# Four small statistic tiles of a two-layer attention and mixture kernel are given 128 bytes a partition each

## The chip, the cores and the metric

The kernel runs on one core of a Trainium2 chip. The metric is the time of one execution on the device in microseconds (us), and lower is better.

## The reference

Attention over 4 batches, 8 heads, 576 positions and 64 features; four heads see a local window of 32 positions, the other four every 32nd position. Its result, 2304 tokens by 512 features, goes through two gated layers of width 1536.

```python
scores = scale * np.matmul(q, k.transpose(0, 1, 3, 2))
scores = np.where(masks[None, :, :, :], scores, -1000000000.0)
attn = np.exp(scores - np.max(scores, axis=-1, keepdims=True))
attn = attn / (np.sum(attn, axis=-1, keepdims=True) + 1e-09)
x = np.matmul(attn, v)                  # then as 2304 tokens x 512
...
x = (x @ w_a) * (x @ w_b) @ w_out       # first layer, "moe"
gate = 1.0 / (1.0 + np.exp(-(x @ w_gate)))
out = gate * (x @ w_val) @ w_out        # second layer, "moe2"
```

## The kernel before, in words

**Precision.** Matmuls of the two layers run on fp32 words in one pass. Each operand is split into a high and a low part, and a product is three matmuls: high by high, low by high, high by low.

**Memory.** Almost all of the on-chip memory is cut into 17 zones (`REGIONS`, L68 to L73): `w0` to `w11` of 12,288 bytes a partition, `x12` to `x15` of 8,192, `h16` of 4,096. The function `at` (L364) gives each zone a tile of its own, and a zone is used anew in three phases; the names in the profile are `w4p` and so on, without the number of the phase. One large tile, `rest` (L361), holds everything else of size. The statistic tiles `nm0`, `nm1`, `nm2` (negated row maxima and sums of the local heads, L573) and `sm0` (the same of the strided heads, L799) are small tiles of their own, made by `buf` (L383). Tiles stand in a partition in the order in which the program first asks for them.

**First part, about 24 to 510 us.** Five tiles of tokens: four of 512 columns (4 batches by 128 positions) and a last one of 256. The tokens of a tile lie in `x12` to `x15` and are the moving operand; block k of the first layer's weights (k = 0 to 11, 128 hidden features each) lies in zone `wk` and is the stationary one. For each tile and each k the engine runs 24 matmuls at L923 (the products with `w_a` and `w_b`) and, one block later, 12 at L1013 (the output product, which moves the hidden values in `h16`). The same zone's weights are loaded for each matmul anew. Between them stand the small matmuls and transposes of the next tile's attention (L563, L604, L618, L877), whose operands lie in `rest`. The strided heads are computed by VectorE alone (L781, L787, L844, L851); the results are transposed at L877 and written to `x13` and `x15`.

**Second part, about 510 us to the end.** The second layer is done in products of 2 by 2 blocks with seven multiplications instead of eight (`seven`, L1276). All its matmuls are at L1292, with 384 columns. In its first stage tokens and their sums in `w0` to `w3`, `w6` to `w9`, `w11` to `w15` and others are moving, weights in `w4`, `w5`, `w10` and `w3` are stationary; in its last stage the zones change parts again, with weights in `w3`, `w4`, `w5`, `w7`, `w10` and `x12` to `x15`.

**Order.** A planner (`Plan`, with costs and due times) writes the instructions of each engine in a fixed order when the program is built. It knows zones and rings by number, and not the size of a small tile or an address.

```python
v = tiles[r][1][:, a - r[0]:a - r[0] + n]                            # L376, at(): a place in a zone
return sb.tile(shape, dtype, tag=f"{ring}{s}", name=f"{ring}{s}")    # L387, buf(): nm0 to nm2, sm0
```

Of the kernel before, what the change touches and what calls it, by code (L numbers as in the profile page):

```python
# [18 lines left out]
HL = H // 2  # L19
# [3 lines left out]
P = 128  # L23
# [322 lines left out]
def attention_moe_kernel(ctx, tc, qkv, sq, sk, sv, w1, w2, mask, ident, out):  # L346
# [17 lines left out]
    def at(a, n, phase=FIRST, dtype=F32):  # L364
        r = region_of(a)
        if r is None:
            v = rest[:, a - F0:a - F0 + n]
        else:
            if tiles.get(r, (None,))[0] != phase:
                name = f"{('w', 'x', 'h')[(r[0] >= X0) + (r[0] >= H0)]}{REGIONS.index(r)}"  # L370
                tiles[r] = phase, sb.tile([P, r[1]], F32, tag=name, name=f"{name}p{phase}")
            v = tiles[r][1][:, a - r[0]:a - r[0] + n]
        return v if dtype == F32 else v.bitcast(dtype)
# [9 lines left out]
    def buf(op, ring, shape, dtype=F32):  # L383
        s = op.slot[ring][0]
        if ring in PLACE:
            return at(PLACE[ring] + s * RINGS[ring][1], shape[1], FIRST, dtype)
        return sb.tile(shape, dtype, tag=f"{ring}{s}", name=f"{ring}{s}")  # L387
# [136 lines left out]
    def attention(g, key, banks, first, war, load=(), held=None, last=True):  # L524
# [44 lines left out]
        def blocks(a):  # L569
            return a.rearrange("p (b k) -> p b k", b=g.nb)  # L570

        def top(op):
            nm = buf(op, "nm", [P, 2 * HL])  # L573
            x["nm"], x["sm"] = nm[:, :g.nb], nm[:, HL:HL + g.nb]
            DVE.tensor_reduce(out=x["nm"], in_=blocks(x["s"]), op=ALU.max, axis=AX.X)  # L575
            DVE.tensor_scalar_mul(x["nm"], x["nm"], -SCALE)  # L576
# [81 lines left out]
        else:  # L658
            a = add("PE", nb * 162, qk, [lq, z] + war, key, take=ring(("c", es)), free=ring(("qk", lq)))
        used(a, [eq, ek])  # L660
        b = add("DVE", dve(w) + 200, top, [a], key + ST, take=[("nm", (0, 1, 2))])
        c = add("ACT", nb * (act(WB) + 186), exp, [b], key + 2 * ST,
                free=[("bank", z)])
# [29 lines left out]
    def strided(i, key, length, start, war):  # L693
        first = i == 0
        tq, t0 = TILES[i] // STRIDE, i * TB // STRIDE
# [100 lines left out]
                reds.append(reads(add("DVE", dve(nh * n * D), reduce, [m, fi], w, free=free), m))  # L796

        def stat(op):
            return buf(op, "sm", [P, HL * 4])[:, :HL * tq]  # L799

        def wide(a):
            return a.unsqueeze(2).to_broadcast([P, HL * tq, n1])
# [1 line left out]
        def top(op):  # L804
            x["m"] = stat(op)
            DVE.tensor_reduce(out=x["m"], in_=s3(), op=ALU.max, axis=AX.X)
# [787 lines left out]
```

## Time and profile before

| | |
|---|---|
| runs | 914.01 us (median of 3; 913.92 to 914.92) |
| span of the profiled execution | 912.5 us, first to last instruction |
| TensorE matmul busy | 903.8 us, 99% |
| TensorE weight load busy | 806.1 us, 88% |
| VectorE busy | 655.6 us, 72% |
| ScalarE busy | 404.7 us, 44% |
| granted TensorE clock | 1.000 of full speed over the whole run |

For the profiled execution the page gives its span alone, and no time of its own; 914.01 - 912.5 = 1.5 us of a run lie outside the span. Matmuls overlap one another, so the record of one is longer than the step from its start to the start of the next: that step is what a stream of matmuls costs, and it is read from rows that give a start, a length and a count.

### The profile page before, as it was taken

What the parts mean: (1) busy time and instruction counts of PE and PEld (TensorE: products, weight loads), DVE (VectorE), ACT (ScalarE), POOL (GpSimd) and SP (SyncE); (2) the same over time, 40 slices, a digit from 0 to 9 for tenths busy, and PEclk for the clock granted to TensorE, in tenths of its full rate; (3) what the DMA queues carried; (4) which work ended last, traced back from release to release, by engine and by line L of the source; (5) the groups of instructions that cost most, each with busy time, mean ns of one, the idle gap of its engine ahead of it and who ended that gap; (6) DMA issues with size and microseconds to landing.
All of it is one profiled execution on the core that took longest, in us unless ns stands there. A gap on an engine that the chain in (4) does not pass through costs nothing.

```text
span 912.5 us, 13664 instructions
## 1 busy us (share of the span) xinstructions
PE 903.8 (99%) x5170; PEld 806.1 (88%) x5170; DVE 655.6 (72%) x1078; ACT 404.7 (44%) x843; POOL 11.8 (1%) x23
## 2 busy tenths in 40 slices
PE   8999999999999999999999999999999999999998
PEld 4678887888888887888899999999999999999998
DVE  7999988998999879811328886675768458659481
ACT  5775644411242113311236655564656445435351
POOL 4000000000000000000000000000000000000000
PEclk9999999999999999999999999999999999999999
DMA  9666564311342123300034333645574588953401
GB/s 318 197 228 220 189 195 137 90 44 59 85 136 71 53 64 119 118 1 1 0 117 148 106 123 114 226 149 186 196 242 162 198 292 323 386 165 114 165 16 62
DMA packets 62513, 132.67 MB, mean 145 GB/s; under 512 B 5872, under 2 KB 37232, under 8 KB 61552
## 3 DMA queue, kind: packets, MB, share of 16 engines
q1 hardware_dynamic: 62160, 131.60, 42.9%
q8 instruction: 40, 0.66, 0.3%
q14 instruction: 25, 0.20, 0.1%
q10 hardware_dynamic: 288, 0.21, 0.1%
HBM read 97.19 MB, written 34.60 MB: 144 GB/s over the span
## 4 chain that ended last, share of the span: by engine, by line
PE 96%; DVE 3%; DMA 0%; issue 0%; ACT 0%; SPq 0%; DVEq 0%
PE bank L1292 43%; PE bank L923 33%; PE bank L1013 17%; PE bank L618 1%; PE bank L563 1%; PE bank L604 1%; DMA w11p<-sk 0%; PE bank L877 0%; DVE s L787 0%; DVE nm L575 0%; DVE rest L491 0%; DVE w11p L781 0%; DVE w8p L851 0%; DVE w9p L851 0%; DVE x14p L630 0%
## 5 line engine op out<-in xcount | busy, mean ns | idle before, releaser
L947 ACT CAST h16p<-rest 128x512 fp32r<-128x512 f32 (+1 forms) x60 | 34.7, 578 | 149.0 <-PE bank L1013 142.9
L1304 DVE TENSOR_TENSOR rest<-bank,rest 128x384 f32<-128x384 f32 x84 | 46.2, 555 | 58.4 <-PE bank L1292 33.5
L943 DVE TENSOR_TENSOR rest<-bank,rest 128x512 f32<-128x512 f32 (+1 forms) x60 | 38.1, 635 | 57.0 <-PE bank L923 56.3
L1065 ACT COPY rest<-bank 128x512 f32<-128x512 f32 (+1 forms) x60 | 32.6, 543 | 95.7 <-PE bank L923 95.5
L1310 ACT COPY rest<-bank 128x384 f32<-128x384 f32 x84 | 40.1, 479 | 69.3 <-PE bank L1292 69.2
L951 DVE TENSOR_TENSOR h16p<-rest,h16p 128x512 fp32r<-128x512 f32 (+1 forms) x60 | 38.2, 636 | 32.7 <-PE bank L1013 27.6
L844 DVE TENSOR_TENSOR rest<-rest,s 128x320 f32<-128x320 f32 (+13 forms) x56 | 51.5, 920 | 0.9
L781 DVE TENSOR_TENSOR rest<-rest 128x320 f32<-128x320 f32 (+13 forms) x56 | 51.5, 919 | 0.9
L787 DVE TENSOR_REDUCE s<-rest 128x5 f32<-128x320 f32 (+13 forms) x56 | 51.2, 914 | 1.2
L851 DVE TENSOR_REDUCE rest<-rest 128x64 f32<-128x320 f32 (+13 forms) x56 | 51.2, 914 | 1.0
L1202 DVE SCALAR_TENSOR_TENSOR rest<-rest 128x512 uint32<-128x512 uint32 x36 | 24.6, 687 | 9.5 <-ACT rest L1195 9.4
L482 ACT ACTIVATE rest<-rest 128x512 f16<-128x512 bf16 x36 | 28.4, 793 | 6.8 <-DMA rest<-w 6.4
L1195 ACT ACTIVATE rest<-rest 128x512 f16<-128x512 bf16 x36 | 28.0, 790 | 4.9 <-DMA rest<-w 4.8
L1375 DVE TENSOR_TENSOR rest<-bank,rest 128x384 f32<-128x384 f32 x36 | 20.0, 556 | 12.2 <-PE bank L1292 11.4
L1314 ACT COPY bank<-bank 128x384 f32<-128x384 f32 x42 | 19.5, 465 | 19.6 <-PE bank L1292 19.1
L1369 ACT ACTIVATE rest<-bank 128x384 f32<-128x384 f32 x36 | 17.7, 491 | 23.2 <-PE bank L1292 23.2
L491 DVE SCALAR_TENSOR_TENSOR rest<-rest 128x512 uint32<-128x512 uint32 x36 | 24.4, 684 | 0.9 <-ACT rest L482 0.9
L581 ACT ACTIVATE rest<-bank,nm 128x96 f32<-128x96 f32 x56 | 18.3, 339 | 12.0 <-DVE nm L576 10.4
L1369 ACT ACTIVATE rest<-rest 128x768 f32<-128x768 f32 x18 | 15.2, 845 | 14.0 <-DVE rest L1304 13.7
L1292 PE MATMUL bank<-w8p,w10p 128*128 128x384 f32 x100 | 20.8, 335 | 0.0
L1292 PEld LDWEIGHTS bank<-w8p,w10p 128*128 128x128 f32 x100 | 17.7, 188 | 0.0
L1292 PE MATMUL bank<-x15p,w3p 128*128 128x384 f32 x88 | 17.6, 335 | 0.0
(500 smaller groups left out, 2426.9 us busy)
## 6 DMA issues: line engine op xcount, KB each, us to landing
rest<-w SPq DMA_DIRECT2D x72, 511.8 KB, 4.0
h2d<-rest SPq DMA_DIRECT2D x18, 768.0 KB, 4.1
rest<-qkv SPq DMA_DIRECT2D x12, 416.0 KB, 4.0
w2p<-h2d SPq DMA_DIRECT2D x12, 384.0 KB, 4.3
w0p<-h2d SPq DMA_DIRECT2D x12, 384.0 KB, 5.4
w1p<-h2d SPq DMA_DIRECT2D x12, 384.0 KB, 4.9
out<-rest SPq DMA_DIRECT2D x24, 192.0 KB, 1.8
x2d<-rest SPq DMA_DIRECT2D x16, 256.0 KB, 2.0
```

The costliest lines, as they stand in the source:

```text
L781: engine[op.eng].tensor_tensor(out=product(op, n), in0=x["k", h][:, :, :n, :], in1=x["q"][h // 2][:, e:e + nh, j:j + 1, :].to_broadcast([P ...
L787: DVE.tensor_reduce(out=weights_of(h, j, n), in_=x["p", op.deps[0]], op=ALU.add, axis=AX.X)
L844: engine[op.eng].tensor_tensor(out=product(op, n, "p (h d t) -> p h d t"), in0=x["v", h][:, :, :, :n], in1=weights_of(h, j, n).unsqueeze(2 ...
L851: DVE.tensor_reduce(out=xs[:, j, e:e + nh, :], in_=x["p", op.deps[0]], op=ALU.add, axis=AX.X)
L923: PE.matmul(x[tag][:, :n], ww[:, c * P:(c + 1) * P], xx(c), start=(u == 0 and c == chunks[0]), stop=(u == last and c == chunks[-1]),)
L943: DVE.tensor_tensor(out=x["g"], in0=x["b"][:, :n], in1=x["g"], op=ALU.mult)
L947: ACT.copy(out=x["hh"], in_=x["g"])
L951: DVE.tensor_tensor(out=x["hl"], in0=x["g"], in1=r32(x["hh"]), op=ALU.subtract)
L1013: PE.matmul(ps[:, :n], ww[:, m * P:(m + 1) * P], x[xx], start=start, stop=stop)
L1292: PE.matmul(bank_of(where), at(*lhs(a, (0, 1, 0)[q], c), F32R), at(*rhs(b, (0, 0, 1)[q], c), F32R), start=p in OPENS and (q, c) == units[0 ...
L1304: DVE.tensor_tensor(out=at(*o), in0=bank_of("Z"), in1=at(*a), op=ALU.add)
L1310: "ACT", act2(NS), lambda op: ACT.copy(out=at(*o), in_=bank_of("Y")), [ops[after]], key - 20))
```

## The change

The four small tiles are asked for with 32 words (128 bytes) a partition: `nm0` to `nm2` had 8 words (32 bytes), `sm0` had 16 (64 bytes). The parts of them that are used stay the same.

```diff
         def top(op):
-            nm = buf(op, "nm", [P, 2 * HL])
+            nm = buf(op, "nm", [P, 32])
             x["nm"], x["sm"] = nm[:, :g.nb], nm[:, HL:HL + g.nb]
...
         def stat(op):
-            return buf(op, "sm", [P, HL * 4])[:, :HL * tq]
+            return buf(op, "sm", [P, 32])[:, :HL * tq]
```

The instructions of every engine are the same in both programs, in the same order (PE, DVE, ACT, POOL and SP alike). What differs is where tiles begin. Byte addresses within a partition, of the built programs:

| tile | before | after | before, modulo 128 | after, modulo 128 |
|---|---|---|---|---|
| rest | 3072 | 3072 | 0 | 0 |
| w11, w10, w9, w7, w6, w8, w5 | 43392 to 117120, in this order, in steps of 12288 | same | 0 | 0 |
| nm0 | 129408 | 129408 | 0 | 0 |
| nm1 | 129440 | 129536 | 32 | 0 |
| sm0 | 129472 | 129664 | 64 | 0 |
| nm2 | 129536 | 129792 | 0 | 0 |
| w4 | 129568 | 129920 | 32 | 0 |
| x12, x14, x13, x15 | 141856 to 166432, steps of 8192 | 352 bytes more | 32 | 0 |
| w0, w1 | 174624, 186912 | 352 bytes more | 32 | 0 |
| h16 | 199200 | 199552 | 32 | 0 |
| w2, w3 | 203296, 215584 | 352 bytes more | 32 | 0 |

Every operand of L923, L1013 and L1292 begins at its zone's start plus a multiple of 512 bytes, so it has its zone's remainder.

## Rows read from the trace of the kernel before

**Rows 1.** The page, part 1: busy time, share of the span, instructions.
```profile
PE 903.8 (99%) x5170; PEld 806.1 (88%) x5170; DVE 655.6 (72%) x1078; ACT 404.7 (44%) x843; POOL 11.8 (1%) x23
```

**Rows 2.** The page, part 4: the chain that ended last, by engine and line.
```profile
PE 96%; DVE 3%; DMA 0%; issue 0%; ACT 0%; SPq 0%; DVEq 0%
PE bank L1292 43%; PE bank L923 33%; PE bank L1013 17%; PE bank L618 1%; PE bank L563 1%; PE bank L604 1%; DMA w11p<-sk 0%; PE bank L877 0%; DVE s L787 0%; DVE nm L575 0%; DVE rest L491 0%; DVE w11p L781 0%; DVE w8p L851 0%; DVE w9p L851 0%; DVE x14p L630 0%
```

**Rows 3.** Line L1013, 195 to 455 us: min/median/max ns, first and last start.
```profile
L1013 PE MATMUL bank<-h16p,w8p x36: 392/397/400, 222.4 to 438.4; 128*128 128x512 f32 x36
...
L1013 PE MATMUL bank<-h16p,w0p x24: 389/389/499, 258.7 to 368.6; 128*128 128x512 f32 x24
...
L1013 PE MATMUL bank<-h16p,w3p x24: 389/389/392, 286.9 to 396.1; 128*128 128x512 f32 x24
```

**Rows 4.** The chain in order of time, third tile: start us, us, what.
```profile
222.56 2.81 PE bank L1013 x12
225.37 5.63 PE bank L923 x24
...
271.68 5.44 PE bank L923 x24
...
287.06 2.72 PE bank L1013 x12
```

**Rows 5.** Line L1013, 457 to 508 us, the tile of 256 columns.
```profile
L1013 PE MATMUL bank<-h16p,w3p x12: 283/283/283, 477.2 to 478.6; 128*128 128x256 f32 x12
...
L1013 PE MATMUL bank<-h16p,w8p x12: 277/280/282, 498.4 to 499.7; 128*128 128x256 f32 x12
```

**Rows 6.** The chain in order of time, the tile of 256 columns.
```profile
474.52 2.88 PE bank L923 x24
477.40 1.44 PE bank L1013 x12
...
498.58 1.41 PE bank L1013 x12
499.98 2.82 PE bank L923 x24
```

**Rows 7.** Groups by form, 565 to 910 us: out<-moving,stationary xcount | busy us, mean ns.
```profile
L1292 PE MATMUL bank<-w8p,w10p 128*128 128x384 f32 x100 | 20.8, 335 | 0.0
L1292 PE MATMUL bank<-w9p,w4p 128*128 128x384 f32 x82 | 16.3, 339 | 0.0
L1292 PE MATMUL bank<-x15p,w3p 128*128 128x384 f32 x76 | 15.3, 335 | 0.0
...
L1292 PE MATMUL bank<-w6p,w5p 128*128 128x384 f32 x72 | 14.5, 336 | 0.0
...
L1292 PE MATMUL bank<-w0p,w10p 128*128 128x384 f32 x36 | 7.2, 336 | 0.0
```

**Rows 8.** Timeline of PE, 705 to 708 us: start us, us, what.
```profile
705.10 1.20 PE L1292 MATMUL bank<-w8p,w10p 128*128 128x384 f32 x6
706.14 1.23 PE L1292 MATMUL bank<-w8p,w4p 128*128 128x384 f32 x6
707.20 1.20 PE L1292 MATMUL bank<-w8p,w10p 128*128 128x384 f32 x6
```

**Rows 9.** The chain in order of time, the second part.
```profile
510.58 44.14 PE bank L1292 x252
559.58 349.59 PE bank L1292 x1996
```

**Rows 10.** Timeline of DVE before the second tile's transposes: start, us, what, [idle].
```profile
125.45 0.69 DVE L951 TENSOR_TENSOR h16p<-rest,h16p 128x512 fp32r<-128x512 f32 x1 [0.79 <-PE bank L1013]
...
131.01 0.69 DVE L943 TENSOR_TENSOR rest<-bank,rest 128x512 f32<-128x512 f32 x1 [0.22 <-PE bank L923]
131.62 0.68 DVE L851 TENSOR_REDUCE rest<-rest 128x64 f32<-128x512 f32 x1
```

**Rows 11.** Timeline of PE at those transposes.
```profile
132.68 0.60 PE L877 MATMUL bank<-idt,rest 128*128 128x128 f32 x4
```

**Rows 12.** Timeline of PE, 558 to 560 us.
```profile
558.32 0.62 PE L1292 MATMUL bank<-w2p,w4p 128*128 128x384 f32 x2 [0.48 <-ACT w4p L1245]
559.58 0.97 PE L1292 MATMUL bank<-w2p,w4p 128*128 128x384 f32 x4 [0.64 <-DVE w4p L1248]
```

## The prediction

> **What bounds the kernel now.** I read the busy times first: the matmul engine is busy for 99% of the span and VectorE for 72% [rows 1]. The chain that ended last says the same with an order: 96% of it is PE, and three lines, L1292, L923 and L1013, make 93% [rows 2]. So the time is a number of matmuls times the step from one to the next, and an edit matters if it changes that step. This edit removes, adds and moves no instruction; it moves addresses. The question is thus whether the trace of before shows a step that depends on the address. It can, since before it holds both kinds of zone: `w5` to `w11` begin at a multiple of 128 bytes ("on 0"), all zones from `w4` on, by place, 32 bytes past one ("on 32").
>
> The first look is at one line with one moving operand. At L1013 `h16` (on 32) moves through weights of every zone, 512 columns each. With weights on 32 the record of a matmul lasts 389 ns at its median, which is also its minimum; with weights on 0 it lasts 397 [rows 3]. The records overlap, so I check the step itself in the chain: twelve matmuls with `w8` take 2.81 us, 234.2 ns each, and twelve with `w3` 2.72 us, 226.7 each; the blocks of 24 at L923 take 5.63 and 5.44 us, 234.6 and 226.7 [rows 4]. (Which block is which follows from the order: an output block at L1013 stands between the products of the next two blocks. The row at 222.56 is that of `w8`, by rows 3, so the 24 behind it belong to `w10`; the row at 287.06 is that of `w3`, and the 24 at 271.68 are its products.) **Pairs of unlike remainder cost 7.5 ns more here.**
>
> With 256 columns it is the other way, by less: `w3` 283 ns and `w8` 280 [rows 5], in the chain 1.44 and 1.41 us for twelve, 2.88 and 2.82 for 24: 120.0 against 117.5 each [rows 6].
>
> Line L1292, 384 columns, has all four combinations. Both on 0: 335 and 336 ns; moving on 0, weights on 32: 339; both on 32: 335; moving on 32, weights on 0: 336 [rows 7]. The steps: six `w8`,`w10` (both on 0) begin 1.04 us before the next six, 173.3 each; six `w8`,`w4` (0 and 32) take 1.06, 176.7 [rows 8].
>
> Pairs of **like** remainder thus step by 120.0, 173.3 and 226.7 ns at 256, 384 and 512 columns: 53.3 and 53.4 more for each 128, or 0.417 ns a column, which is a cycle of the level of 2.4 GHz that was granted all along. Taken from the steps, the columns leave 13.3 ns at every width. For **unlike** pairs the same columns leave 10.8, 16.7 and 20.9: a rest that grows with the width. My reading is that the two streams the engine reads, moving columns and the next weights, hinder each other by an amount that depends on where they stand to each other, not on either one alone. After the change all pairs are alike.
>
> **The sum.** The counts come from the loops.
> - 512 columns, unlike before: 4 tiles x 7 blocks (`w5` to `w11`) x 36 matmuls = 1008. They go from 234.2 to what like pairs take, 226.7 in undisturbed blocks. Blocks that stand by attention matmuls are not so clean, so I count 227.5: 6.7 x 1008 = **6.8 us gained** (bounds: 3.0 if only what parts the fastest records, 392 and 389 in rows 3, is gained; 7.6 at 226.7).
> - 512 columns, like before (both on 32): 4 x 5 x 36 = 720. They go to both on 0, a pair that 512 columns never show. I take no change. Bounds: at 384 columns the two like pairs differ by at most 1 ns in the forms shown [rows 7], so 0.7 us either way.
> - 256 columns, unlike before: 7 x 36 = 252, from 117.5 to 120.0: **0.6 us lost** (bounds 0 to 0.6).
> - 384 columns: the long stretch of L1292 is 1996 matmuls in 349.59 us, 175.15 each over all four combinations [rows 9]; both on 0 is 173.3 in a clean run. Of these 1.8 ns I leave 0.5 for stragglers (forms with both on 0 range from 335 to 336). 1.3 x 2268 (18 groups of 84 and 6 of 126) = **2.9 us gained** (bounds 0.4 to 4.1).
> - The small tiles: a maximum, an exponential and a reciprocal read the same few words of them as before. Nothing is added to them; they are hidden behind PE's 99% in any case.
> - The matmuls of attention (L563, L604, L618, L877) read `rest`, which stays where it is, save for the first tile's: nothing.
>
> Together 6.8 - 0.6 + 2.9 = 9.1 us. Against the profiled execution: 912.5 - 9.1 = 903.4 of span; with the 1.5 us outside it, 904.9. The runs' median is 914.0, and 914.0 - 9.1 gives the same. A difference under 0.2% (1.8 us) can't be told from none.
>
> **Does all of it reach the end?** PE waits little now, so I look for what is only just in time. The tightest place is the second tile's transposes: VectorE's last reduction ends at 131.62 + 0.68 = 132.30, and PE begins the transposes at 132.68 [rows 10, 11]. PE would come there some 1.5 us earlier (228 unlike matmuls of blocks 5 to 11 before it, at 6.7). But VectorE waits for PE itself on the way, for 0.79 us at 125.45 and 0.22 at 131.01 [rows 10]: what it waits for comes earlier too, so it moves along, and I count no loss. If it did not, the loss would be 1.5 - 0.4 = 1.1 us there. PE's 1.1 us of waits at 558 us [rows 12] are for weights that are written into `w4`, which an earlier PE reads free earlier; they stay.
>
> One rule speaks against the change. The rows show a step that differs by 7.5 ns with nothing but the weights' zone changed [rows 3, 4]. The Trainium skill, page "TensorE: Matmul & The Clock Gate", section "Step-by-step: what each phase is for", says that the engine has two independent read ports, and that loading the next weights takes no read bandwidth from the running matmul. By that rule the sum would be zero, and the trace disagrees with it as far as these rows go.
>
> **Rivals.**
> - *No change, 914.0.* The difference between zones is real but is not their remainder: `w5` to `w11` are also the zones at lower addresses, and all zones on 32 lie above them. If it is the distance, or the side of memory, that slows a pair, 352 bytes change nothing. For it: in the trace remainder and side go together. Against it: `w4` follows `w5` almost directly in memory and behaves like `w3` at the far end; and unlike pairs are faster at 256 columns. The skill's rule above would also end here. Chance 0.08.
> - *Slower, 916.1.* In the first part both moving operands are always on 32, so the rows there can't tell "like" from "weights on 0 are slow whatever moves". If the latter holds, all 1728 matmuls with 512 columns take 234.2: the 720 lose 7.5 each, 5.4 us, the 1008 gain nothing, the 180 with 256 columns that are on 32 now gain 2.5 each, 0.4 us, and L1292 still gains 2.9, since its rows show both on 0 as fastest. 914.0 + 5.4 - 0.4 - 2.9 = 916.1. It decides as soon as the weights' remainder alone sets the step. Against it: at 384 columns weights on 0 are the faster ones when the moving operand is on 0 (335 against 339, rows 7). Chance 0.04.
> - *VectorE becomes the bound of the first tiles, 908.* Its strided attention fills most of 36 to 133 us. If it did not move along with PE at this and the following tiles, some 3 us of the gain up to about 250 us would turn into waits before L877: 904.9 + 3 = 908. Chance 0.04.
> - *The forecast*: like pairs cost 13.3 ns over their columns, 904.9. Chance 0.84.
>
> **The numbers.** The bounds of the terms give a gain of 3.0 - 0.7 - 0.6 + 0.4 = 2.1 us at the one end (911.9) and 7.6 + 0.7 + 4.1 = 12.4 at the other (901.6). That all terms lie at the same end is unlikely: 902.0 to 909.0 takes in VectorE's rival and leaves out the 0.12 of the first two rivals and a little on either side. Faster by more than 0.2%: 0.84 + 0.04 less a little, 0.87; within 0.2%: 0.08; slower: 0.05.
>
> **What would show it.** In the profile after: at L1013 all blocks `w0` to `w11` at about 389 ns with 512 columns and 283 with 256, without a seam between `w4` and `w5`; in the chain 2.72 us for each twelve and 5.44 to 5.48 for each 24; the long stretch of L1292 at 173.8 ns a matmul, about 347 us; VectorE's share a little up. Wrong would be: the seam still there (no change); all blocks at 397 (slower); blocks at 389 with new waits of PE for L851 at L877 (VectorE). Of the steps I am least sure of the pair on 0 at 512 columns, which no row shows.

## The result

The change is faster: 904.11 us (median of 4 runs, 903.51 to 905.05) against 914.46 us (913.92 to 915.07) for the kernel before on the same chip, a ratio of 0.9883 with a 95% interval of 0.9871 to 0.9894. The forecast was 904.9, the range 902.0 to 909.0. A second time, in the last set of runs, the change gave 904.32 us and 0.9888 (0.9871 to 0.9904).

The span of the profiled execution fell from 912.5 to 901.7 us, 10.8 us less. The first part of the page after the change:

```profile
PE 893.2 (99%) x5170; PEld 802.6 (89%) x5170; DVE 654.9 (73%) x1078; ACT 405.7 (45%) x843; POOL 11.7 (1%) x23
```

PE is busy for 10.6 us less, the same instructions as before, while VectorE and ScalarE work as long as they did [rows 1]. The time thus came out of the matmuls themselves. Line L1013 from 195 to 455 us (minimum, median and maximum in ns, first and last start), the answer to [rows 3]:

```profile
L1013 PE MATMUL bank<-h16p,w8p x36: 389/389/389, 219.0 to 431.3; 128*128 128x512 f32 x36
...
L1013 PE MATMUL bank<-h16p,w0p x24: 389/389/497, 254.6 to 362.7; 128*128 128x512 f32 x24
...
L1013 PE MATMUL bank<-h16p,w3p x24: 389/389/392, 282.8 to 390.3; 128*128 128x512 f32 x24
```

Block 8, which lasted 397 ns, now lasts 389 like the others, and its fastest and slowest record are the same. The chain in order of time shows the step (start us, us, what), beside [rows 4]:

```profile
219.15 2.72 PE bank L1013 x12
221.87 5.44 PE bank L923 x24
...
267.55 5.44 PE bank L923 x24
...
282.93 2.72 PE bank L1013 x12
```

All blocks shown step by 226.7 ns; the seam between `w4` and `w5` is gone. With 256 columns it went the other way, as [rows 5, 6] had it: block 8 takes 1.44 us for twelve matmuls instead of 1.41. The chain there (block 6, then block 8):

```profile
482.70 1.44 PE bank L1013 x12
...
491.34 1.44 PE bank L1013 x12
```

L1292 by form, 557 to 902 us (out<-moving,stationary xcount | busy us, mean ns), beside [rows 7], and its two stretches in the chain, beside [rows 9]:

```profile
L1292 PE MATMUL bank<-w8p,w10p 128*128 128x384 f32 x100 | 20.7, 334 | 0.0
L1292 PE MATMUL bank<-w9p,w4p 128*128 128x384 f32 x82 | 16.0, 334 | 0.0
L1292 PE MATMUL bank<-x15p,w3p 128*128 128x384 f32 x76 | 15.3, 334 | 0.0
...
L1292 PE MATMUL bank<-w0p,w10p 128*128 128x384 f32 x36 | 7.2, 334 | 0.0
```

```profile
503.58 43.69 PE bank L1292 x252
552.12 346.28 PE bank L1292 x1996
```

Every form now has the same mean, where they ran from 335 to 339, and the long stretch takes 173.49 ns a matmul (346.28 / 1996) instead of 175.15.

The tightest hand-over did not become a wait. VectorE's last reduction and PE's transposes for the second tile, beside [rows 10, 11], in the timelines of the two engines:

```profile
129.75 0.68 DVE L851 TENSOR_REDUCE rest<-rest 128x64 f32<-128x512 f32 x1
```

```profile
130.75 0.60 PE L877 MATMUL bank<-idt,rest 128*128 128x128 f32 x4
```

PE comes 1.93 us earlier (132.68 before), VectorE's end 1.87 us earlier (132.30 before, 130.43 now), and no idle time stands in PE's row. The waits for `w4` stay as they were, 0.48 and 0.64 us [rows 12]:

```profile
550.87 0.62 PE L1292 MATMUL bank<-w2p,w4p 128*128 128x384 f32 x2 [0.48 <-ACT w4p L1245]
552.12 0.96 PE L1292 MATMUL bank<-w2p,w4p 128*128 128x384 f32 x4 [0.64 <-DVE w4p L1248]
```

### The profile page after: what moved, and what is told of

It is laid out like the page before. It is cut to its first block, busy times and chain, and to the rows that moved or that the text cites. A ratio compares the mean times of both kernels' runs of the same rounds, so it can differ in the third digit from the quotient of the medians.

```text
span 901.7 us, 13664 instructions
## 1 busy us (share of the span) xinstructions
PE 893.2 (99%) x5170; PEld 802.6 (89%) x5170; DVE 654.9 (73%) x1078; ACT 405.7 (45%) x843; POOL 11.7 (1%) x23
## 4 chain that ended last, share of the span: by engine, by line
PE 96%; DVE 3%; DMA 0%; ACT 0%; issue 0%; DVEq 0%
PE bank L1292 43%; PE bank L923 32%; PE bank L1013 16%; PE idle L423 1%; PE bank L563 1%; PE bank L618 1%; PE bank L604 1%; DMA rest<-w 0%; PE bank L877 0%; DVE rest L491 0%; PE bank L436 0%; DVE w8p L851 0%; DVE w9p L851 0%; DVE nm L575 0%; DVE x14p L630 0%
## 5 line engine op out<-in xcount | busy, mean ns | idle before, releaser
L581 ACT ACTIVATE rest<-bank,nm 128x96 f32<-128x96 f32 x56 | 18.3, 339 | 12.2 <-DVE nm L576 10.6
L1292 PE MATMUL bank<-w8p,w10p 128*128 128x384 f32 x100 | 20.7, 334 | 0.0
L1375 DVE TENSOR_TENSOR rest<-rest 128x768 f32<-128x768 f32 x18 | 17.2, 953 | 0.7 <-ACT rest L1369 0.2
L1292 PEld LDWEIGHTS bank<-w8p,w10p 128*128 128x128 f32 x100 | 17.6, 188 | 0.0
```

The source lines that it names most:

```text
L1292: PE.matmul(bank_of(where), at(*lhs(a, (0, 1, 0)[q], c), F32R), at(*rhs(b, (0, 0, 1)[q], c), F32R), start=p in OPENS and (q, c) == units[0 ...
L1375: DVE.tensor_tensor(out=at(*o), in0=src(), in1=at(*o), op=ALU.mult)
```

## Experiments

The forecast came true, but that shows the size and not the reason. Left open were: whether the small tiles or the zones count; whether each operand's own place counts or only their distance; and with what period.

**sm40: another way to the same remainders.** Of the small tiles only `sm0` grows, to 160 bytes.

```diff
-            return buf(op, "sm", [P, HL * 4])[:, :HL * tq]
+            return buf(op, "sm", [P, 40])[:, :HL * tq]
```

Expected: 

> The statistic tiles nm0 to nm2 stay at 32 bytes, sm0 alone grows to 160 bytes: the zones behind them move by 96 bytes instead of 352, and all zones begin on 0. If the remainder of the zones is what counts, the time is that of the change, 904.1 us within 1 us, and every block at L1013 lasts 389 ns with 512 columns. If something about the small tiles themselves were what counts (rows of 128 bytes each), the time stays at 914.

Measured: 905.08 us (903.76 to 907.61), 0.9900 of before (0.9879 to 0.9921). Line L1013:

```profile
L1013 PE MATMUL bank<-h16p,w5p x36: 389/389/389, 196.4 to 409.0; 128*128 128x512 f32 x36
```

The rows of the three `nm` tiles are 32 bytes as before, and the gain is there: the zones count, not the small tiles. (`sm0` itself did grow here; in apart128, below, it grows further and most of the gain is gone.)

**all32: every zone on 32.** The change, with a tile ahead of all zones widened by 32 bytes.

```diff
-    nil = sb.tile([P, P], BF16, name="nil")
+    nil = sb.tile([P, P + 16], BF16, name="nil")[:, :P]
```

Expected: 

> The change, and a small tile ahead of all zones widened by 32 bytes: every zone stands on 32, none on 0. If only the place of the two streams to each other counts, the time is 904.1 within 1 us and every block at L1013 lasts 389 ns. If each operand pays for not standing on a multiple of 128, the time is 914 or more (all 4428 matmuls would pay).

Measured: 903.57 us (903.42 to 905.15), 0.9885 (0.9869 to 0.9902). Line L1013 and the long stretch of L1292:

```profile
L1013 PE MATMUL bank<-h16p,w8p x36: 389/389/389, 219.1 to 431.3; 128*128 128x512 f32 x36
...
L1013 PE MATMUL bank<-h16p,w3p x24: 389/389/391, 282.8 to 390.2; 128*128 128x512 f32 x24
```

```profile
552.16 346.27 PE bank L1292 x1996
```

No zone stands on a multiple of 128, and the rows shown are those of the change. Standing on a multiple of 128 is worth nothing by itself; standing alike is.

**nm_only: half of the change.** `nm` has 32 words, `sm` its old 16; zones from `w4` on move to 64.

Expected: 

> Half of the change: nm0 to nm2 take 128 bytes, sm0 keeps 64. All zones from w4 on stand on 64, w5 to w11 on 0. If two streams are alike when their remainders modulo 64 agree, all pairs are alike and the time is 904.1. If they must agree modulo 128, the pairs of w5 to w11 with h16 and x stay unlike, their step at 512 columns stays near 234 and the time near 914.

Measured: 912.17 us (911.83 to 914.26), 0.9977 (0.9968 to 0.9987). Line L1013:

```profile
L1013 PE MATMUL bank<-h16p,w8p x36: 393/396/398, 221.7 to 437.2; 128*128 128x512 f32 x36
...
L1013 PE MATMUL bank<-h16p,w3p x24: 388/389/397, 286.1 to 395.1; 128*128 128x512 f32 x24
```

With 512 columns 64 is not alike: the seam is there, nearly as high as at 32 (396 against 397). Still the time is 2.0 us below that of before, clear of the noise. About half of that comes from L1292, which takes 1.0 us less over the long stretch than the 349.59 of before:

```profile
558.44 348.57 PE bank L1292 x1996
```

So not every unlike pair costs the same; the maps below show which do.

**mov32: the dose doubled.** Each zone may lead by some words, so that it stands where it is wanted; all weights on 0, tokens and hidden values on 32.

```diff
-                tiles[r] = phase, sb.tile([P, r[1]], F32, tag=name, name=f"{name}p{phase}")
+                size = r[1] + -(-LEAD_OF[name] // 8) * 8
+                tiles[r] = phase, sb.tile([P, size], F32, tag=name, name=f"{name}p{phase}")[:, LEAD_OF[name]:]
```

Expected: 

> The dose doubled in the first part: all weight zones on 0, x12 to x15 and h16 on 32, so every pair of L923 and L1013 is unlike (720 more than before). By the theory of unlike pairs every block at L1013 lasts 397 ns with 512 columns and 280 with 256, also w0 to w4 that lasted 389 before. Against the change: 1728 x 6.6 = 11.4 us more, 432 x 2.5 = 1.1 less, and some of L1292's pairs with x zones unlike, about 1 us: 915 to 916. If the side of memory counted, w0 to w4 would stay at 389 and the time at 914 or below.

Measured: 914.53 us in one run, beside 914.59 for before. L1013 is L1015 in this file:

```profile
L1015 PE MATMUL bank<-h16p,w8p x36: 391/394/401, 223.8 to 441.0; 128*128 128x512 f32 x36
...
L1015 PE MATMUL bank<-h16p,w3p x24: 392/397/400, 288.9 to 398.8; 128*128 128x512 f32 x24
```

`w3`, whose address differs by no more than a few hundred bytes from before, goes from 389 to 397. On which side of memory a zone lies does not explain that. The time decides nothing: it is 0.5 to 1.5 us below the bounds that were given and 0.5 above what the side of memory allowed, in a single run, where those of before range from 913.70 to 915.62. The rows decide. Their medians lie between 394 and 398 and not all at 397.

**apart128: a multiple of 128 everywhere, and still not alike.** `sm0` takes 288 bytes (72 words): all zones stand on multiples of 128, but `w5` to `w11` 128 and the others 0 modulo 256. In the change all of them are 128 modulo 256.

Expected: 

> nm0 to nm2 as before, sm0 takes 288 bytes: every zone begins on a multiple of 128, as in the change, but w5 to w11 are 128 modulo 256 and all zones from w4 on 0 modulo 256. If agreeing modulo 128 is enough, as the prediction had it, the time is that of the change, 904 within 1 us. If the distance counts modulo 256, as the second map says, the pairs that were unlike before are unlike again: at L1292 (1080 of them) they step by about 176 instead of 173.3, 2.9 us more; the 1008 with 512 columns are not in a map, anything from 226.7 to 234: 907 to 914.

Measured: 913.42 us (912.90 to 915.61), 0.9989 (0.9979 to 0.9998). Line L1013 and the long stretch of L1292:

```profile
L1013 PE MATMUL bank<-h16p,w8p x36: 390/392/404, 222.1 to 437.3; 128*128 128x512 f32 x36
...
L1013 PE MATMUL bank<-h16p,w3p x24: 389/389/396, 286.6 to 395.3; 128*128 128x512 f32 x24
```

```profile
558.81 349.68 PE bank L1292 x1996
```

This is the run that corrects the prediction's reason. The long stretch is back at 175.2 ns (349.68 / 1996) and nine tenths of the gain is gone. **To agree modulo 128 is not enough; the distance counts modulo 256.** The change itself gained because its 352 bytes happened to make the two groups of zones agree modulo 256 too.

**map16 and map512: the step by itself.** Two kernels that only multiply. Each pair of places gets 28 (24) matmuls in a row, with the weights' slices 512 bytes apart as in the kernel. The core of the second:

```python
FULL = [(m, m + d) for m in (0, 2, 4, 6) for d in range(0, 128, 4)]   # words; moving, weights
...
for c in range(COUNT):
    a, o = w + c % 12 * P, m + c % 4 * n
    PE.matmul(ps[:, :n], wts[:, a:a + P].bitcast(F32R), mov[:, o:o + n].bitcast(F32R), ...)
```

Expected of the first: 

> The disputed step by itself: the kernel computes nothing of the reference; it runs 28 matmuls for each of 64 pairs of remainders (moving 0 to 112 and weights 0 to 112 in steps of 16 bytes), with 512 and 384 columns in two orders and with 256 in one. By the theory of like pairs the step settles at 226.7, 173.3 and 120.0 ns wherever both remainders agree, whatever they are; where they differ by 32 it settles at about 234, 175 and 117.5. By the rival that the place of either operand alone counts, the pairs on the diagonal differ among themselves by several ns. In the sweep a pair of moving 16 and weights 80 ran at 170 for 384 columns; whether that is a settled step is read here.

Expected of the second: 

> Nothing of the reference is computed: 24 matmuls for each pair of a moving operand on 0, 8, 16 or 24 and weights 0 to 496 bytes behind it in steps of 16, with 384 columns; the same for 0 and 16 with 256 columns; both in rising and in falling order. If the distance counts modulo 128, each row repeats four times within 0.5 ns. If it counts modulo 256, the step of 113.3 at a distance of 64 comes back at 320 but not at 192 and 448. If the state that the pair before left behind decides, rising and falling order give different steps for the same pair, and then no single table of distances holds; the first map showed this at 384 columns for distances 64 and -64.

Measured: 1696.72 and 1473.99 us in one run each, which is the length of the list. The steps below are differences of the starts of successive records in the trace, the mean of the last 12 of a pair, in ns. In map512 the table repeats after 256 bytes, within 0.4 ns but for seven places, all in falling order (the very first pair of the list left out), and it does not repeat after 128. One of the two halves is shown:

```
weights behind moving (bytes, mod 256)     0    16    32    48    64    80    96   112   128   144   160   176   192   208   224   240
moving  0, 384 columns, rising order   173.3 173.3 173.3 173.3 173.3 176.2 173.3 173.3 176.4 177.2 176.7 173.3 173.3 175.6 176.7 173.3
moving 16, 384 columns, rising order   175.6 180.0 176.7 176.7 173.3 175.8 175.6 174.7 176.7 173.3 175.6 173.3 170.0 175.0 176.0 175.6
moving 16, 384 columns, falling order  175.5 180.0 176.7 176.7 173.3 176.2 175.5 174.7 176.7 173.3 175.6 173.3 176.7 173.3 176.0 175.6
moving  0, 256 columns, rising order   120.0 118.6 118.6 117.8 113.3 118.8 117.2 120.4 120.0 118.3 120.0 118.2 117.8 116.7 116.7 120.0
moving  0, 256 columns, falling order  120.3 117.9 118.2 118.3 117.8 118.5 118.6 119.4 118.8 120.0 120.0 118.1 117.8 116.7 116.7 116.9
moving 16, 256 columns, rising order   118.3 117.4 120.0 119.5 113.3 119.2 117.8 113.3 120.3 113.3 120.0 120.0 118.3 118.3 118.3 116.7
```

Four things are to be seen.

- Distance 0 with the moving operand on 0 gives 173.3 and 120.0, as in the kernel. In these two kernels nearly nothing but TensorE works (VectorE 1.6 and ScalarE 5.0 of 1472 us in map512), so the differences do not come from what other engines read or write at the same time.
- Distance 0 is not the only good one. With 384 columns ten of the sixteen distances in the first row settle at 173.3. Of the two unlike distances of before, 160 (moving on 0, weights on 32) is slow, 176.7, and 96 (moving on 32, weights on 0) is not. [Rows 7] have the same order: 339 ns for the one, 336 for the other, and 335 to 336 for like pairs.
- The moving operand's own place counts after all: on 16 even distance 0 is slower (175.6). In map16 the places 0, 32, 64 and 96 give much the same rows, and so do 16, 48, 80 and 112: it counts modulo 32.
- At some places the pair that ran before decides. Distance 192 with moving 16 gives 170.0 in rising order and 176.7 in falling; 448, the same modulo 256, gives 170.0 in both. The two streams settle in one of several rhythms.

With 512 columns map16 settles at 226.7 for like pairs on 0, 32, 64 and 96, at 230.0 to 233.3 for those on 16, 48, 80 and 112, and, with moving on 0, at 233.3 for distances 32 and 64 and 234.2 for 96, which is the step of the unlike pairs of before. So its expectation was wrong twice: "wherever both remainders agree, whatever they are" fails off the multiples of 32, and with 384 columns distance 32 settles at 173.3 and not at 175.

**sweep0: a miss that held the answer.** Tokens and hidden values on 0 modulo 128, the weight zones `w0` to `w11` each on another place.

Expected: 

> Moving operands of the first part on 0, the weight zones on 0, 16, 32, 48, 64, 80, 96, 112, 4, 8, 120 and 0 (w0 to w11). By the theory of like pairs w0 and w11 step by 227 ns with 512 columns and 120 with 256; w2 (32) by 234 and 117.5. If 64 is the period, w4 steps like w0, w6 like w2 and w5 like w1. By the rival that a smaller unit counts (16 bytes), w1 to w7 all step by 227 and only 4, 8 and 120 differ. The time should lie between 904 and 915.

Measured: 916.16 us in one run, beyond the bounds. The zone that should have been untouched, `w0`, was not (L1015 is L1013 here; `w2` is on 32):

```profile
L1015 PE MATMUL bank<-h16p,w0p x24: 390/393/497, 259.7 to 369.5; 128*128 128x512 f32 x24
...
L1015 PE MATMUL bank<-h16p,w2p x24: 388/396/501, 278.5 to 388.3; 128*128 128x512 f32 x24
```

The addresses of the built program say why. Modulo 256, `h16` stands on 0 here and `w0` and the tokens on 128. So `w0` agrees with the tokens and is 128 away from the hidden values: the distance that apart128 tests. The steps of one block each show it, from the starts in the trace in ns, `w0` with the tokens (L925) and with `h16` (L1015):

```
230 236 228 233 231 226 227 318 335 231 236 228 233 231 227 227 226 227 227 226 227 227 226 227
234 234 232 232 228 230 233 241 232 231 232 230
```

The first comes back to 226 and 227 each time, the second does not. The row that missed shows the period of 256, before anyone looked for it. (The time, 1.2 us beyond the bounds, is not taken apart here.)

The first block also shows that like pairs have to settle, here in five steps after a block of unlike ones. (The 318 and the 335 stand beside attention matmuls, whose own steps are left out here and below.) After transposes it can take longer. In a block of `w8` at L923 in the changed kernel four transposes of L877 stand between the 231 and the 314, and nine steps later the rhythm of 680 ns for three is back:

```
226 227 227 226 227 227 226 227 227 226 227 231 314 235 233 236 224 231 236 228 233 231 226 227
```

In sweep0 blocks at different distances follow one another all the time, so it can't serve as a table of distances, which is why the maps were made.

**last32 and last112: a version that beats both.** Like pairs are at the smallest step seen with 512 columns, but not with 256. The last tile leaves room in its zones, so its tokens and hidden values can stand further in, by `PUT` words (8, then 28), while all else stays as in the change.

```diff
-        o = (i % 2) * N2
+        o = (i % 2) * N2 + PUT[i]              # PUT = [0, 0, 0, 0, 28]
...
-            x["hh"] = buf(op, "hh", [P, N2], F32R)[:, :n]
+            x["hh"] = buf(op, "hh", [P, N2], F32R)[:, (n < N2) * 28:][:, :n]
```

Expected of last32: 

> The change, and the tokens and hidden values of the last tile (256 columns) are put 32 bytes further into their zones: its 432 matmuls become unlike, all others stay alike. By the rows of before an unlike pair with 256 columns steps by 117.5 instead of 120.0: 432 x 2.5 = 1.1 us less than the change, 903.0. If like pairs were best at every width, it stays at 904.1 or grows.

Expected of last112: 

> The change, with the last tile's tokens and hidden values 112 bytes further into their zones: weights then stand 144 bytes behind the moving operand (modulo 256), which itself is 16 past a multiple of 32. The second map settles there at 113.3 ns with 256 columns in both orders, against 120.0 for like pairs: 432 x 6.7 = 2.9 us less than the change, 901.2. If the real mix of blocks and waits keeps it from settling, it lies at 116 to 118 and the gain at 1 to 1.7 us.

Expected of the change beside it: 

> The change once more, as it is, beside the last two kernels on the same chip: 904.1 within 0.6 us, 1.1 to 1.2% below the kernel before.

Measured: last32 903.49 us, 0.9878 (0.9862 to 0.9895); last112 902.06 us, 0.9862 (0.9847 to 0.9877); the change beside last112 904.32 us, 0.9888. The chain of last32 in its last tile:

```profile
471.86 2.80 PE bank L924 x24
474.66 1.40 PE bank L1014 x12
```

Its steps are 116.7 ns: weights stand 224 behind the moving operand modulo 256, where map512 has 116.7 with moving on 0. By its time alone last32 can't be told from the change, which did not run beside it on that chip. The chain of last112 in its last tile (L924 and L1014 are L923 and L1013):

```profile
475.88 2.72 PE bank L924 x24
478.60 1.36 PE bank L1014 x12
479.96 2.72 PE bank L924 x24
482.68 1.36 PE bank L1014 x12
```

Its steps are 113.3 ns (2.72 / 24), where the change has 120.0 and before 117.5 or 120.0. 432 x 6.7 = 2.9 us were expected and 904.32 - 902.06 = 2.3 were measured; medians of one kernel differ by up to 0.4 (914.16 to 914.59 for before). Summed over their steps in the trace, the 432 take 49.39 us in last112 and 52.11 in the change beside it: 2.7 less. The intervals of last112 and of the change overlap, so that last112 beats the change rests on its rows; that it beats the kernel before is clear.

Not tried: to bring the 2268 matmuls of L1292 from 173.3 to 170.0 ns, by estimate 7.5 us less. That place (moving on 16, weights 192 behind) needs another lead for the second part than for the first. Whether it would hold among other pairs is open: in one of its four turns in map512 (distance 192 and 448, two orders) it settled at 176.7.

## Why the prediction was right, and where its reason was not

**What bounds the kernel** and **the step depends on the place of the weights**: right. The rule of the Trainium skill that spoke against it (page "TensorE: Matmul & The Clock Gate", section "Step-by-step: what each phase is for", two independent read ports) does not account for this step: in mov32 the same matmul with `w3` went from 389 to 397 ns with nothing but addresses changed. What in the chip makes the step depend on them, no run here shows.

**The terms.** Measured from the chain, from its first row of products to the first row of L1292 and from there to the end:
- The first part ran from 29.63 to 510.58 us before and from 29.44 to 503.58 after: 480.95 and 474.14, 6.8 us gained. Forecast were 6.8 - 0.6 = 6.2. Summed over their steps in the trace, the 1008 unlike matmuls with 512 columns took 237.49 us before and 230.55 after: 6.9 gained. The 252 with 256 columns lost 0.7, about as said. What was missing is the term that I put at nothing, the 720 like pairs: 170.41 us before and 169.87 after, 0.5 gained. Some 0.2 of that is in blocks that stand right behind an unlike one before the change and have to settle there. 0.3 is one wait for ScalarE in the profile of before, which the profile of after doesn't have:

```profile
149.47 0.19 PEld L1013 LDWEIGHTS bank<-h16p,w0p 128*128 128x128 f32 x1 [0.46 <-ACT rest L987]
```

- The second part: 44.14 + 349.59 = 393.73 before, 43.69 + 346.28 = 389.97 after, 3.8 us gained where 2.9 were forecast. I left 0.5 ns for stragglers; in a stretch where all pairs are alike there are nearly none (all forms at 334). By the starts in the trace, like pairs stepped by 174.4 ns before, those at distance 96 by 175.0 and those at 160 by 176.8, and by 173.4 all after: like pairs among unlike ones lost too, and about half of the gain is that of distance 160.
- The start, up to the first chain row of products, was 0.2 us shorter. It differs between executions of one kernel: it was 30.98 in the second profile of the change.

6.8 + 3.8 + 0.2 = 10.8 us, the difference of the spans.

**The waits**: right. VectorE moved along with PE, as the two rows of it show.

**The reason**: half right. "An amount that depends on where they stand to each other, not on either one alone" holds at multiples of 32 (all32, map16), and fails at 8, 16 and 24 (map512). The step that failed is the remainder: the prediction took like to mean alike modulo 128. The table of before could not tell, since its two groups stand on 128 and 32 modulo 256, which is 0 and 32 modulo 128. apart128 shows 256. The word "unlike" was too coarse as well: with 384 columns many unlike distances settle at the step of like pairs, and the 336 in the prediction's own rows was a sign of it.

That the forecast was met is in part luck. Had the change added 224 bytes instead of 352, as apart128 does, every sentence of the forecast would have read the same, and the time would have been 913.4. The single number of 13.3 ns for like pairs was read rightly, but it is not what the columns leave at best: the smallest steps seen are 113.3, 170.0 and 226.7.

**The rivals.** "No change, by the side of memory" falls by the result, and by apart128, which has the sides of the change and nearly the time of before. "Weights on 0 are slow whatever moves" falls by block 8 at 389 ns with weights on 0. "VectorE becomes the bound" falls by the hand-over at 130.75.

## What to carry to other kernels

Where a stream of matmuls is the bound and each loads its weights anew, group the records by the zones of their operands before anything else: a seam of 2% between zones with equal instructions was a matter of addresses here. Compare the distance of the two operands modulo 256 in the built program, and not the roundness of each address. A small tile that is asked for between large ones moves all that come after it, so a change of its size may move the time without touching the work: here by 1.1% (the change) or by 0.1% (apart128).

## What the runs showed of the hardware that was not expected

- The step of a matmul that loads 128 columns of fp32 weights depends on the distance between moving operand and weights, with a period of 256 bytes (map512, apart128), and on the moving operand's place modulo 32 (map16). With 256 columns it lies between 113.3 and 120.4 ns in map512, with 384 between 170.0 and 180.7, at the full clock.
- Equal remainders modulo 256 are not best at every width: on multiples of 32 they give 226.7 ns with 512 columns, the smallest step seen there, and 120.0 with 256, near the largest (map16, map512).
- It is a rhythm that settles: like pairs return to 226.7 ns about nine steps after a disturbance by transposes, and for some pairs what ran before decides which rhythm is reached (170.0 or 176.7 ns in map512).
- The smallest settled steps, 113.3, 170.0 and 226.7 ns for 256, 384 and 512 columns, are each 17/16 of what the columns take at 0.417 ns (106.7, 160.0, 213.3). No pair in the maps went below.
